# An attention and feed-forward kernel: one weight row loaded between the two loads of x, the first projection begun on half of the tiles, and the tiles of x evacuated by halves on two engines

## The chip, the cores and the metric

One core of a Trainium2 chip. The time is the device time of one execution in microseconds (us). The kernel is long tuned: about 287 us, of which the change touches the first fifteen. Medians and ranges are of all runs (one of the kernel before, 290.98 us, counts as slow). A ratio is the mean time of one kernel's fast runs over the mean of the other's fast runs of the same rounds, so it is not quite the ratio of the medians that are quoted.

## The reference

```python
# x: (1, 2048, 640) bf16; 32 heads of 20; F = 1728
qkv = x @ wqkv                                   # (640, 1920): q, k, v
pq, pk = q @ w_phi, k @ w_phi                    # by head, 20 x 20
phi = concat(softmax(p), softmax(-p))            # for q and k
kv, z = phi_k^T @ v, sum(phi_k)
a = (phi_q @ kv) / (phi_q @ z + 1e-6) @ wo
b = (gelu(x @ w_gate) * (x @ w_up)) @ w_down
g = sigmoid((x * gate_w).sum(-1))
out = g * a + (1 - g) * b
```

## The kernel before

TensorE needs x transposed (`xT`, 16 tiles of 128 tokens). The first four tiles are loaded as they are (`xtok`, two loads of two tiles) and transposed on TensorE into PSUM, from where VectorE and ScalarE copy ("evacuate") them to `xT`; the other twelve are transposed by the DMA engines. Then v is projected for these four tiles, one "v step" per tile and row block of the weights (five row blocks `w3[:, kt]`, each 160 KB, called v rows here). After that come v of tiles 4 and 5, the folding of `w_phi` into the weights of k and q, and everything else.

```python
# loads(): all on one queue (SyncE), in this order
        xload("sp", 0)                      # tiles 0 and 1, 320 KB
        xload("sp", 2)                      # tiles 2 and 3, 320 KB
        for kt in range(KD):                # v rows 0 to 4, 160 KB each
            sc.dma("sp", lambda e: e.dma_start(self.w3[:, kt, 0:D], w3[:, kt, 2 * D:3 * D]), writes=[("wv", kt)])
        xturn(4, 2)                         # DMA transposes: x tiles 4, 5
        wload(self.wkT, D, "wkT")           # k's weights
        xturn(6, 2)                         # x tiles 6, 7
        wload(self.wqT, 0, "wqT")
# x_transpose(t, ek): ten 64-row transposes, then ONE evacuation by DVE or ACT
        if ek == "a":
            sc.op("act", lambda e: e.activation(out, src, AF.Copy), reads=rd, writes=[("xT", t)])
        else:
            sc.op("dve", lambda e: e.tensor_copy(out, src), reads=rd, writes=[("xT", t)])
# attention_state(): TensorE's order
        for n in (512, 512, 512, 512, 512, 512, 128, 128, 128):
            ...                             # dummy matmuls until x lands
        xt(0, "d"); xt(1, "a")
        ...                                 # six dummy matmuls
        xt(2, "d"); xt(3, "a")
        for kt in range(4):                 # (written out in the kernel)
            for t in range(4):
                vs(t, kt)
        self.blockdiag()
        self.gate_column(6)
        for t in range(4):
            vs(t, 4)
            ...                             # evacuate v: 480 columns per tile, tails together
        ve(4, 6); ve(5, 0)                  # v of tiles 4, 5
        f(0, "k", (2, 3), "d"); f(1, "k", (4, 5), "a")   # folds of k ...
```

The softmax here doesn't subtract the row's maximum and nothing guards it: scores larger than these inputs give would overflow.

Of the kernel before, what the change touches and what calls it, by code (L numbers as in the profile page):

```python
# [3 lines left out]
P = 128  # L4
BF16 = mybir.dt.bfloat16
F32 = mybir.dt.float32
AF = mybir.ActivationFunctionType
# [100 lines left out]
class _Kernel:  # L108
    S, D, H, DH, F = 2048, 640, 32, 20, 1728
    KD = D // P  # L110
# [97 lines left out]
    def loads(self):  # L208
        sc, nc = self.sc, self.nc
        D, KD, DH, P_ = self.D, self.KD, self.DH, P  # L210
        w3 = self.wqkv.rearrange("(kt p) n -> p kt n", p=P)
# [3 lines left out]
        def xload(q, j):  # L215
            sc.dma(q, lambda e: e.dma_start(self.xtok[:, j:j + 2, :], x4[:, j:j + 2, :]),
                   writes=[("xtok", j), ("xtok", j + 1)])

        def wload(T, c0, key):
            sc.dma("sp", lambda e: e.dma_start_transpose(T[:, :, :], self.wqkv[:, c0:c0 + D]), writes=[key])  # L220

        def xturn(t, n):
# [5 lines left out]
              writes=["gtmp"])  # L228
# [2 lines left out]
                                                compare_op=ALU.not_equal, fill=1.0, base=0, channel_multiplier=1),  # L231
              writes=["ident"])
        xload("sp", 0)
        xload("sp", 2)
        for kt in range(KD):
            sc.dma("sp", lambda e: e.dma_start(self.w3[:, kt, 0:D], w3[:, kt, 2 * D:3 * D]), writes=[("wv", kt)])
        xturn(4, 2)
        wload(self.wkT, D, "wkT")
        xturn(6, 2)
        wload(self.wqT, 0, "wqT")  # L240
        xturn(8, 4)
        xturn(12, 4)
# [11 lines left out]
        for r in (0, 1):  # L254
            sc.dma("sp", lambda e: e.dma_start(self.wd_sb[64 * r:64 * r + 64, 13, :], self.wd[13 * P:self.F, :]),
                   writes=[("wd13", r)])
        sc.dma("sp", lambda e: e.dma_start(self.wo_sb[:, :, :], self.wo.rearrange("(kt p) n -> p kt n", p=P)),
               writes=["wo"])
# [3 lines left out]
        for i in range(KD):  # L262
            n = self.HHI[i] - self.HLO[i] + 1
# [11 lines left out]
            reads=[("mask", 1)], writes=["wphi"])  # L275
# [10 lines left out]
        for s in range(self.NSV):  # L286
            pool(lambda e, s=s: e.memset(self.vaug[:, s, :, DH:self.DA], 1.0), [("vone", s)])

    def x_transpose(self, t, ek):

        sc = self.sc
        b, w = (0, 4, 2, 6)[t], self.D // 2
        bks = (b, b + 1)
        pv = self.bank(b, 1024).bitcast(BF16).rearrange("p (r c) -> p r c", r=2)[:, :, 0:w]
        for c in range(self.KD):
            for r in (0, 1):
                a = 64 * r
                sc.op("pe", lambda e: e.transpose(  # L298
                    pv[:, r, c * 64:(c + 1) * 64], self.xtok[a:a + 64, t, c * P:(c + 1) * P],
                    self.ident[a:a + 64, a:a + 64]),  # L300
                    reads=[("xtok", t), "ident"], writes=[("ps", bks[r])], signal=(c == self.KD - 1))
        out = self.xT[:, :, t * P:(t + 1) * P].rearrange("p c (r t) -> p c r t", t=64)
        src = pv.rearrange("p r (c t) -> p c r t", t=64)
        rd = [("ps", b) for b in bks]
        if ek == "a":
            sc.op("act", lambda e: e.activation(out, src, AF.Copy), reads=rd, writes=[("xT", t)])
        else:
            sc.op("dve", lambda e: e.tensor_copy(out, src), reads=rd, writes=[("xT", t)])

    def blockdiag(self):  # L310
        DH = self.DH
# [56 lines left out]
                    kt == self.KD - 1, [("xT", t)] + [(k, kt) if k != "wgate" else k for k in keys])  # L368

    def v_step(self, t, kt):  # L370
        sc = self.sc
        for c0, n, bk, col in ((0, 480, t, 0), (480, 160, 4 + t // 3, 160 * (t % 3))):
            sc.op("pe", lambda e, c0=c0, n=n, bk=bk, col=col: e.matmul(  # L373
                self.bank(bk)[:, col:col + n], self.xT[:, kt, t * P:(t + 1) * P], self.w3[:, kt, c0:c0 + n],
                start=(kt == 0 and col == 0), stop=(kt == self.KD - 1), skip_group_check=True),
                reads=[("xT", t), ("wv", kt)], writes=[("ps", bk)], signal=(kt == self.KD - 1))

    def v_first_evac(self, ts, ek, tail):
        sv, nt = ts[0], len(ts)
        h0, nh = (24, 8) if tail else (0, 24)  # L380
        dst = self.vaug[:, sv:sv + nt, h0:h0 + nh, 0:self.DH]
        bk = 4 + ts[0] // 3 if tail else ts[0]
        src = self.bank(bk, nt * nh * self.DH).rearrange("p (t h d) -> p t h d", t=nt, d=self.DH)
        rd = [("ps", bk)] + [("vone", t) for t in ts]
        wr = [("vaug", t) if tail else ("vmain", t) for t in ts]
        if ek == "d":
            self.sc.op("dve", lambda e: e.tensor_copy(dst, src), reads=rd, writes=wr)
        else:
            self.sc.op("act", lambda e: e.activation(dst, src, AF.Copy), reads=rd, writes=wr)

    def k_early(self, t, b0):
        self.proj(t, 640, 384, b0, 128, ["wk2"])
# [70 lines left out]
    def gram(self, t):  # L463
        sc = self.sc
        se, sv = t % self.NSE, t % self.NSV
        va = self.vaug[:, sv, :, :].rearrange("p h c -> p (h c)")
        for g, a, b, c, lo, f0, nf in self.gram_groups():
            sc.op("pe", lambda e: e.matmul(  # L468
                self.ps[a:a + 64, b * 512 + c:b * 512 + c + 2 * nf], va[:, lo:lo + 64], self.Ek[:, se, :, f0:f0 + nf],
                start=(t == 0 and g in (0, 1, 8, 9)), stop=(t == self.NT - 1 and g in (6, 7, 9, 10)),  # L470
                skip_group_check=True),
                reads=[("Ek", se, 0), ("Ek", se, 1), ("vaug", sv), ("vmain", sv), ("vone", sv)], writes=[("ps", b)],
                signal=(g in (7, 10)))

    def kv_evac(self):
# [75 lines left out]
    def attention_state(self):  # L551
        NT = self.NT
        order = [(b, i) for b in range(self.NB) for i in range(self.KD)]
        sc = self.sc
        ones = self.nc.const_aps.tensor(1.0, [P, 512], BF16)
        for n in (512, 512, 512, 512, 512, 512, 128, 128, 128):
            sc.op("pe", lambda e: e.matmul(self.bank(0, n), ones[:, 0:P], ones[:, 0:n], start=True, stop=True),  # L557
                  writes=[("ps", 0)])
        vs, ve, xt = self.v_step, self.v_first_evac, self.x_transpose
        xt(0, "d")  # L560
        xt(1, "a")
        for i in range(3):
            for a, b in ((0, 2), (64, 3)):
                sc.op("pe", lambda e: e.matmul(self.bank(b, P), ones[a:a + 64, 0:P], ones[a:a + 64, 0:P], start=True,  # L564
                                               stop=True), writes=[("ps", b)])
        xt(2, "d")
        xt(3, "a")
        for t in range(4):
            vs(t, 0)
        for t in range(4):  # L570
            vs(t, 1)
        for t in range(4):
            vs(t, 2)
        for t in range(4):
            vs(t, 3)
        self.blockdiag()
        self.gate_column(6)
        for t in range(4):
            vs(t, 4)
            ve([t], "ad"[t % 2], False)  # L580
            if t == 2:
                ve([0, 1, 2], "a", True)
        ve([3], "d", True)
        f = self.fold
        ve, ke = self.v_early, self.k_early
        ve(4, 6)
        ve(5, 0)
        f(0, "k", (2, 3), "d")
        f(1, "k", (4, 5), "a")
        f(2, "k", (6, 7), "d")  # L590
        f(3, "k", (0, 1), "a")
        f(4, "k", (2, 3), "d")
        ve(6, 4)
        ke(0, 6)
        self.k_sums(0)
        ve(7, 0)
        ke(1, 2)
        f(0, "q", (4, 5), "d")
        f(1, "q", (6, 7), "d")
        ke(2, 0)  # L600
        f(2, "q", (4, 5), "d")
        f(3, "q", (2, 3), "d")
        self.proj(3, 640, 384, 6, 128, ["wk2"])
        f(4, "q", (4, 5), "d")
        self.proj(3, 1024, 257, 7, 0, ["wk2", "wgate"])
        self.k_evac(3, 6)
        self.k_scale(0)
        self.k_norm(1)
        self.pq(0, 1, 1, 0)
        self.pq(0, 0, 0, 1)  # L610
        self.pq(0, 3, 3, 2)
        self.columns = True
        self.gram(0)
        self.k_norm(2)
        self.pq(0, 2, 2)
        self.k_norm(3)
        n = 4
        g = 1
        for t in range(4, NT):
            if t < 8:  # L620
                self.k_early(t, 1)
            else:
                self.vk(t)
            self.k_norm(t)
            m = 2 * t - 2 if t < 8 else t + 5
            while n < m:
                if n == m - 1:
                    for g in range(g, t - 2):
                        self.gram(g)
                    g = t - 2  # L630
                self.pq(order[n][0], order[n][1], n)
                n += 1
# [83 lines left out]
    def down_pair(self, t0, banks, widths):  # L716
# [63 lines left out]

    NUMB = 2
    oldk = [("Ek", k, r) for k in range(4) for r in (0, 1)] + [(w, k) for w in ("Dk", "Rk") for k in range(4)] + [
        (w, k) for w in ("vaug", "vmain", "vone") for k in range(8)]
    oldw = [(w, k) for w in ("wv", "wk2", "wq2") for k in range(5)] + ["wgate"]

    def ffn(self):
# [88 lines left out]
```

## Time and profile before

| | |
|---|---|
| time, first three runs | 286.37, 287.10, 290.98 us |
| span of the profiled execution (286.25 us) | 285.0 us |
| TensorE busy | 281.1 us |
| first v step | 5.28 us |
| first fold of k | 13.54 us |

The page of the kernel before; the first lines are busy time with its share of the span, the last ones the chain of work that ended last, by engine and by line:

```profile
span 285.0 us, 7066 instructions
PE 281.1 (99%) x3045; PEld 186.1 (65%) x3060; DVE 174.4 (61%) x352; ACT 105.2 (37%) x200; POOL 5.3 (2%) x36
...
PE 99%; issue 0%; ACT 0%
PE ps L361 62%; PE ps L737 28%; PE ps L681 2%; PE ps L373 2%; PE ps L468 2%; PE ps L341 1%; PE ps L557 1%; PE ps L298 0%; ACT outsb L750 0%; PE ps L564 0%; PE ps L323 0%
```

TensorE (PE) is the chain.

The timeline of TensorE in the opening of the kernel before. Columns: start, duration, engine, line, operation, what it writes and reads, shapes, how many merged into the row, and in brackets the idle time before it with what ended it:

```profile
3.81 0.71 PE L298 MATMUL ps<-ident,xtok 64*128 64x64 bf16 x20
4.34 0.51 PE L564 MATMUL ps<-const-bfloat16-1.0 64*128 64x128 bf16 x6
4.70 0.53 PE L298 MATMUL ps<-ident,xtok 64*128 64x64 bf16 x20
5.28 4.56 PE L373 MATMUL ps<-w,xT 128*128 128x480 bf16 x32
```

Transposes of tiles 0 and 1 at 3.81, dummies, transposes of tiles 2 and 3 at 4.70, v from 5.28: no bracket, so no long wait. And the view of the tile `xtok`, the two loads of x and their times to landing:

```profile
L216 SPq DMA_DIRECT2D xtok<-in_A_x_dram x2: 408/410/413, 0.8 to 1.3; - x2
...
DMA to landing us min/median/max: 2.9/3.2/3.4
```

The first load is issued at 0.80 and lands at 3.72, the second is issued at 1.27 and lands at 4.66 (the landing times of single transfers are in the trace). The v rows land at 5.15, 5.75, 6.32, 6.91 and 7.39.

### The profile page before, as it was taken

To read this page: it belongs to the slowest core of one execution; us is meant where nothing else is said; L and a number is where in the kernel's file an instruction comes from. 1 tells how busy PE (TensorE), PEld (TensorE's weight loads), DVE (VectorE), ACT (ScalarE), POOL (GpSimd) and SP (SyncE) were. 2 spreads that over 40 slices of the span, in tenths; PEclk is the share of its full clock that TensorE was granted. 3 is DMA by queue.
4 is the path that set the end of the run, shared out by engine and by line. 5 is a ranking of instruction groups with operands and counts; after the bars stand their busy time and mean duration, and the time that the engine had idled before them with its cause. 6 is when DMAs were issued, how large, how long until landed. Compare 5 with 4: busy or idle time off the path is not lost.

```text
span 285.0 us, 7066 instructions
## 1 busy us (share of the span) xinstructions
PE 281.1 (99%) x3045; PEld 186.1 (65%) x3060; DVE 174.4 (61%) x352; ACT 105.2 (37%) x200; POOL 5.3 (2%) x36
## 2 busy tenths in 40 slices
PE   8999999999999999999999999999999999999996
PEld 4665799999984444444444444445777777777786
DVE  1459999999976652667242334225883883883801
ACT  4367898667754223222322223221112112112021
POOL 7000000000000000000000000000000000000000
DMA  8999993000002000011000000000233223322421
GB/s 228 225 199 313 361 349 111 2 0 2 2 0 48 0 0 2 2 23 25 0 0 0 2 0 0 0 2 0 26 82 58 50 62 59 70 52 68 71 72 48
DMA packets 36937, 18.67 MB, mean 66 GB/s; under 512 B 28970, under 2 KB 36394, under 8 KB 36906
## 3 DMA queue, kind: packets, MB, share of 16 engines
q1 hardware_dynamic: 36240, 18.19, 26.3%
q8 instruction: 24, 0.39, 0.6%
q10 hardware_dynamic: 666, 0.03, 0.2%
q14 instruction: 7, 0.06, 0.1%
HBM read 9.04 MB, written 2.62 MB: 41 GB/s over the span
## 4 chain that ended last, share of the span: by engine, by line
PE 99%; issue 0%; ACT 0%
PE ps L361 62%; PE ps L737 28%; PE ps L681 2%; PE ps L373 2%; PE ps L468 2%; PE ps L341 1%; PE ps L557 1%; PE ps L298 0%; ACT outsb L750 0%; PE ps L564 0%; PE ps L323 0%
## 5 line engine op out<-in xcount | busy, mean ns | idle before, releaser
L361 PE MATMUL ps<-xT,wg_sb 128*128 128x512 bf16 (+1 forms) x265 | 63.8, 379 | 0.4 <-issue 0.2
L361 PE MATMUL ps<-xT,wu_sb 128*128 128x512 bf16 (+1 forms) x263 | 63.3, 379 | 0.4
L653 ACT ACTIVATE gl<-ps 128x512 bf16<-128x512 f32 x52 | 30.9, 596 | 72.9 <-PE ps L361 70.7
L655 DVE TENSOR_TENSOR hT<-ps,gl 128x512 bf16<-128x512 f32 x39 | 26.6, 689 | 38.8 <-PE ps L361 38.7
L737 PE MATMUL ps<-wd_sb,hT 64*128 64x320 bf16 x648 | 48.5, 296 | 0.0
L361 PEld LDWEIGHTS ps<-xT,wu_sb 128*128 128x128 bf16 (+1 forms) x270 | 26.6, 99 | 29.5
L361 PEld LDWEIGHTS ps<-xT,wg_sb 128*128 128x128 bf16 (+1 forms) x270 | 26.2, 99 | 29.0 <-ACT gl L653 0.2
L361 PE MATMUL ps<-w,xT 128*64 128x512 bf16 (+6 forms) x398 | 41.5, 325 | 0.1
L750 ACT ACTIVATE outsb<-ps,Gm 128x320 bf16<-128x320 f32 (+2 forms) x31 | 14.5, 515 | 72.4 <-PE ps L737 72.4
L737 PEld LDWEIGHTS ps<-wd_sb,hT 64*128 64x128 bf16 x648 | 31.1, 94 | 12.2 <-issue 0.4
L361 PEld LDWEIGHTS ps<-w,xT 128*64 128x64 bf16 (+1 forms) x400 | 35.9, 107 | 4.5
L737 PE MATMUL ps<-wo_sb,goT 64*128 64x320 bf16 (+2 forms) x340 | 26.5, 288 | 0.0
L361 PE MATMUL ps<-xT,wq 128*64 128x512 bf16 (+1 forms) x184 | 26.0, 380 | 0.1
L438 DVE TENSOR_REDUCE Dk<-Ek 128x64 f32<-128x1280 bf16 x16 | 23.7, 1478 | 3.7 <-ACT gcol L426 3.7
L452 DVE TENSOR_TENSOR Ek<-Ek,Dk 128x640 bf16<-128x640 bf16 x32 | 25.0, 821 | 0.6
L708 DVE TENSOR_TENSOR O<-ps,RH 128x640 bf16<-128x640 f32 x32 | 24.7, 815 | 0.0
L423 ACT ACTIVATE Ek<-ps 128x640 bf16<-128x640 f32 x32 | 20.7, 703 | 4.2 <-PE ps L361 4.2
L537 ACT ACTIVATE Eq<-ps 128x512 bf16<-128x512 f32 x40 | 21.6, 607 | 0.6 <-PE ps L361 0.4
L655 DVE TENSOR_TENSOR xT<-ps,gl 128x512 bf16<-128x512 f32 x13 | 9.0, 690 | 18.2 <-PE ps L361 18.2
L737 PEld LDWEIGHTS ps<-wo_sb,goT 64*128 64x128 bf16 x340 | 16.0, 94 | 5.3
L361 PEld LDWEIGHTS ps<-xT,wq 128*64 128x64 bf16 (+1 forms) x185 | 15.4, 108 | 2.9
L737 PE MATMUL ps<-wd_sb,xT 64*128 64x320 bf16 (+2 forms) x270 | 16.0, 269 | 0.0
(71 smaller groups left out, 173.8 us busy)
## 6 DMA issues: line engine op xcount, KB each, us to landing
out_dram<-outsb SPq DMA_DIRECT2D x7, 320.0 KB, 2.3
wd_sb<-in_B_w_down_dram SPq DMA_DIRECT2D x1, 2080.0 KB, 12.9
wg_sb<-in_B_w_gate_dram SPq DMA_DIRECT2D x1, 1120.0 KB, 7.4
wu_sb<-in_B_w_up_dram SPq DMA_DIRECT2D x1, 1120.0 KB, 9.8
wg_sb<-in_B_w_gate_dram SPq DMA_DIRECT2D x1, 960.0 KB, 9.1
wu_sb<-in_B_w_up_dram SPq DMA_DIRECT2D x1, 960.0 KB, 9.3
w<-in_A_wqkv_dram SPq DMA_DIRECT2D x5, 160.0 KB, 3.6
wo_sb<-in_A_wo_dram SPq DMA_DIRECT2D x1, 800.0 KB, 8.5
```

The lines of the kernel that those rows point to most:

```text
L361: self.sc.op("pe", lambda e: e.matmul(self.ps[a:z, bank * 512 + c0:bank * 512 + c0 + n], lhs[:, a:z], rhs, start=first, stop=fin), reads=r ...
L373: sc.op("pe", lambda e, c0=c0, n=n, bk=bk, col=col: e.matmul(self.bank(bk)[:, col:col + n], self.xT[:, kt, t * P:(t + 1) * P], self.w3[:, ...
L423: self.sc.op("act", lambda e, s=s, scale=scale: e.activation(self.Ek[:, se, s, :], self.ps[:, o:o + self.D], AF.Exp, scale=scale), reads=[ ...
L438: sc.op("dve", lambda e: e.tensor_reduce(self.Dk[:, se, 0, :].rearrange("p (s h) -> p s h", h=H), self.Ek[:, se, :, :].rearrange("p s (h d ...
L452: sc.op("dve", lambda e, v=v, r=r: e.tensor_tensor(v, v, r, ALU.mult), reads=[("Rk", se)], writes=[("Ek", se, s)])
L468: sc.op("pe", lambda e: e.matmul(self.ps[a:a + 64, b * 512 + c:b * 512 + c + 2 * nf], va[:, lo:lo + 64], self.Ek[:, se, :, f0:f0 + nf], st ...
L537: sc.op("act", lambda e, s=s, scale=scale: e.activation(self.Eq[:, s, i, b * self.BT:(b + 1) * self.BT], self.bank(bank), AF.Exp, scale=sc ...
L653: sc.op("act", lambda e: e.activation(self.gl[:, slot, :], self.bank(banks[0]), AF.Gelu_apprx_tanh), reads=[("ps", banks[0])], writes=[("g ...
L655: sc.op("dve", lambda e: e.tensor_tensor(hT, self.bank(banks[1]), self.gl[:, slot, :], ALU.mult), reads=[("ps", banks[1]), ("gl", slot)], ...
L708: dve(lambda e, o=o, f=f, s=s: e.tensor_tensor(o, V[s][:, :, :, 0:DH], f, ALU.mult), rb + [key(6 + s)], [("O", s, sl)], guard=old)
L737: sc.op("pe", lambda e: e.matmul(self.bank(bk, w), lhs, rhs, start=opens and x == 0, stop=end and not opens, skip_group_check=True), reads ...
L750: sc.op("act", lambda e: e.activation(dst, self.bank(bk, w), AF.Copy, scale=g), reads=rd, writes=wr)
```

## The change

The intent: do not wait for tiles 2 and 3. v row 0 is loaded between the two loads of x, so that the first v steps of tiles 0 and 1 run while tiles 2 and 3 arrive. Each tile is evacuated in two halves, left on VectorE and right on ScalarE, so that it is ready sooner. Each tile now has its own pair of PSUM banks for v and one evacuation, and the gate column (the weights of the gate `g`, transposed on TensorE and copied into the weights by VectorE) moves behind tile 5, when a bank is free.

```diff
         xload("sp", 0)
+        vload(0)
         xload("sp", 2)
-        for kt in range(KD):
-            sc.dma("sp", ...v row kt...)
+        for kt in range(1, KD):
+            vload(kt)
...
-        if ek == "a":
-            sc.op("act", ...whole tile...)
-        else:
-            sc.op("dve", ...whole tile...)
+        for r in (0, 1):
+            if r:
+                sc.op("act", ...half r..., reads=[("ps", 2 * t + r)], writes=[("xTh", t, r)])
+            else:
+                sc.op("dve", ...half r..., reads=[("ps", 2 * t + r)], writes=[("xTh", t, r)])
...
-        xt(2, "d")
-        xt(3, "a")
-        (v rows 0 to 3, each over tiles 0 to 3)
-        self.blockdiag()
-        self.gate_column(6)
-        (v row 4 with v_first_evac)
+        vs(0, 0)
+        vs(1, 0)
+        xt(2)
+        xt(3)
+        for ts, k in (((0, 1), 1), ((2, 3), 0), ((2, 3), 1), (range(4), 2)):
+            for t in ts:
+                vs(t, k)
+        self.blockdiag()
+        for t in range(4):
+            vs(t, 3)
+            vs(t, 4)
+            self.v_evac(t, 2 * t, "ad"[t % 2])
-        ve(4, 6)
-        ve(5, 0)
+        ve(4, 0)
+        ve(5, 2)
+        self.gate_column(4)
 (the folds and later steps: other bank numbers, same order)
```

## The prediction

> What bounds the kernel now. The chain of waits is 99% TensorE, and the page shows TensorE busy 281.1 of 285.0 us. Any gain must make TensorE start useful work earlier or wait less; what the opening gains or loses should pass to the end. VectorE is about 98% busy from 25 to 77 us (busy time by stretch), but it starts from TensorE's output and shifts with it. The change touches about 3.8 to 15 us.
>
> The opening before (timeline, single instructions, landing times of the DMA issues):
> - x of tiles 0 and 1 lands at 3.72, of tiles 2 and 3 at 4.66; v rows at 5.15, 5.75, 6.32, 6.91, 7.39; the transposed wk at 12.84 and it is first used at 13.49.
> - Transposes of tiles 0, 1: 3.81 to 4.34 (issue). Dummy matmuls to 4.70. Transposes of tiles 2, 3: 4.70 to 5.07 (issue); their spacing falls from 53 to 29 ns at about 4.87, where the fast clock comes on.
> - v starts at 5.28 and its 20 tile-steps (about 0.27 us each, 5.44 in all) end at 10.99, with the gate column's transpose inside. TensorE idles only 0.2 to 0.3 us between 4.70 and 11: no long wait for the change to fill.
>
> What the change does, with durations from the trace:
> - DMA: v row 0 lands at about 4.2 to 4.3, x of tiles 2 and 3 at 5.15, the rest unchanged.
> - Evacuation by halves: VectorE took 0.49 us and ScalarE 0.70 for 640 elements. From other lengths in the trace (ScalarE 0.57 for 480, 0.18 for 1; VectorE 0.18 for 5) a half is an estimated 0.34 on VectorE, 0.44 on ScalarE. ScalarE must do all four right halves. Tile 0 is ready at about 4.85, tile 1 at 5.3 (before: 4.89, 5.36).
> - TensorE: dummies to 4.70; wait 0.2; v(0,0); wait 0.1; v(1,0) to about 5.6; transposes of tiles 2, 3 now all at the fast clock, 0.29 instead of 0.37 to 0.5; row 1 for tiles 0, 1 to 6.45; then tiles 2 and 3 wait for ScalarE's halves, an estimated 0.1 to 0.2 each; end of v about 11.0 to 11.1, against 10.99.
> - So 0.54 us of v moves ahead, but almost all of it is returned as short waits for ScalarE.
> - The gate column's transpose moves behind tile 5 and its VectorE copy (0.18, about 0.5 with the semaphores) now holds bank 4, which fold 1 of k needs some 0.4 us later: an estimated wait of 0.1 to 0.2.
>
> Sum: between 0.3 us earlier and 0.5 later, centre 0.1 to 0.2 later. That is inside the spread of the three runs (286.4, 287.1, and 290.98, likely slow).
>
> Predicted 287.1 us, 80% range 286.2 to 288.1. Faster by over 2%: 1%; within 2%: 98%; slower by over 2%: 1%.
>
> What would show the steps right: v's first matmul at 4.8 to 5.0; new TensorE waits on xT (ScalarE) at the first uses of tiles 1, 2, 3; tile 4's v starting within 0.3 us of 11.0; a short wait of fold 1 for the gate copy; the rest of the trace the same, shifted.
>
> What would make it wrong: the new gaps could keep the clock slow longer. The Trainium skill, "TensorE: Matmul & The Clock Gate", Part 1, says the full clock needs one busy window of about 3.4 us; the trace agrees roughly (matmuls from 0.84, fast at 4.87). [...]

## The result, and the profile after

Median 287.55 us (287.28 to 287.73, six runs) against 286.82 us (286.37 to 290.98, six runs); ratio 1.0028, with a 95% interval of 1.0014 to 1.0041. It is slower beyond the noise, by about 0.8 us between the means of the fast runs. (The medians differ by 0.7 us, the figure used below; that of the kernel before includes its slow run.)

The page of the changed kernel:

```profile
span 286.1 us, 7067 instructions
PE 281.3 (98%) x3044; PEld 185.7 (65%) x3060; DVE 174.8 (61%) x353; ACT 105.2 (37%) x201; POOL 5.3 (2%) x36
...
PE 97%; DMA 2%; issue 1%; SPq 0%; ACT 0%
PE ps L362 63%; PE ps L716 28%; PE ps L660 2%; PE ps L453 2%; DMA xtok<-in_A_x_dram 2%; PE ps L342 1%; PE ps L299 0%; SPq L216 0%; SPq L220 0%; ACT outsb L729 0%; PE ps L324 0%
```

TensorE's busy time is the same. A new name stands in the chain: the load of `xtok` (x of tiles 0 to 3). The chain again, in order of time, up to 12 us (start, duration, what):

```profile
1.73 4.49 DMA xtok<-in_A_x_dram
6.22 0.05 issue
6.27 0.47 PE ps L299 x20
6.73 0.21 issue
6.94 5.09 PE ps L362 x36
```

The second load of x is issued at 1.73 and lands at 6.22. The chain runs through it: everything from 6.27 on waited for it. The timeline of TensorE in the changed kernel:

```profile
3.83 0.72 PE L299 MATMUL ps<-ident,xtok 64*128 64x64 bf16 x20
4.36 0.51 PE L549 MATMUL ps<-const-bfloat16-1.0 64*128 64x128 bf16 x6
4.88 0.81 PE L362 MATMUL ps<-w,xT 128*128 128x512 bf16 x4
6.27 0.47 PE L299 MATMUL ps<-ident,xtok 64*128 64x64 bf16 x20 [0.57 <-DMA xtok<-in_A_x_dram]
6.94 0.44 PE L362 MATMUL ps<-w,xT 128*128 128x128 bf16 x2 [0.21 <-issue]
```

The intent is met: two v steps (four matmuls) run from 4.88, 0.40 us earlier than before. Then the wait of 0.57 us, marked with its cause. (0.57 is counted from the modelled end of the last matmul; from the moment at which a further matmul could have started, 5.53, it is 0.74.) The row at 6.94 seems to wait for "issue"; in truth the record of the 512-column matmul ahead of it is missing, which must have started at about 6.73, just after v row 1 had landed (6.67).

The view of the tile `xtok` in the changed kernel; the maximum is the second load, 1.1 us more than before:

```profile
L216 SPq DMA_DIRECT2D xtok<-in_A_x_dram x2: 412/423/434, 0.8 to 1.7; - x2
...
DMA to landing us min/median/max: 3.0/3.7/4.5
```

| landing, us | before | changed |
|---|---|---|
| x, tiles 0 and 1 | 3.72 | 3.79 |
| v row 0 | 5.15 | 4.15 |
| x, tiles 2 and 3 | 4.66 | 6.22 |
| v rows 1 to 4 | 5.75 to 7.39 | 6.67 to 8.24 |

The account, from single instructions of the two traces: v starts 0.40 us earlier; its first step runs partly at half clock (+0.10); the wait for x of tiles 2 and 3 (+0.74); their transposes now lie within v (+0.27); the wait for v row 1 (+0.15). That is +0.86 us, and the first fold of k starts at 14.43 instead of 13.54 (+0.89). From there the two traces run nearly in parallel (the products `phi_k^T @ v` start at 29.41 and 28.44). In this account the two waits for DMA, 0.89 us together, are the whole loss: without them an estimated 0.03 us would have been gained. So the change had little to win here even with perfect landings, since the transposes that it moves into v take back 0.27 of the 0.40 us. The spans differ by 1.1 us; the last 0.2 us are gathered in two later places that were not traced to a cause. The timed medians differ by 0.7 us rather than 1.1, because the profiled execution of the kernel before (286.25 us) was one of its fastest.

### The profile page after: what moved, and what is told of

It is laid out like the page before. It is cut to its first block, busy times and chain, and to the rows that moved or that the text cites. A ratio compares the mean times of both kernels' runs of the same rounds, so it can differ in the third digit from the quotient of the medians.

```text
span 286.1 us, 7067 instructions
## 1 busy us (share of the span) xinstructions
PE 281.3 (98%) x3044; PEld 185.7 (65%) x3060; DVE 174.8 (61%) x353; ACT 105.2 (37%) x201; POOL 5.3 (2%) x36
## 4 chain that ended last, share of the span: by engine, by line
PE 97%; DMA 2%; issue 1%; SPq 0%; ACT 0%
PE ps L362 63%; PE ps L716 28%; PE ps L660 2%; PE ps L453 2%; DMA xtok<-in_A_x_dram 2%; PE ps L342 1%; PE ps L299 0%; SPq L216 0%; SPq L220 0%; ACT outsb L729 0%; PE ps L324 0%
## 5 line engine op out<-in xcount | busy, mean ns | idle before, releaser
L362 PE MATMUL ps<-w,xT 128*64 128x512 bf16 (+6 forms) x437 | 47.3, 323 | 0.3 <-issue 0.2
L362 PEld LDWEIGHTS ps<-w,xT 128*64 128x64 bf16 (+1 forms) x440 | 38.8, 106 | 7.3 <-issue 0.4
```

The source lines that it names most:

```text
L362: self.sc.op("pe", lambda e: e.matmul(self.ps[a:z, bank * 512 + c0:bank * 512 + c0 + n], lhs[:, a:z], rhs, start=first, stop=fin), reads=r ...
```

## The experiments

Theory A: the loss is the late landing of x of tiles 2 and 3, brought about by the order of the loads. Theory B: it is the halves on ScalarE, the moved gate column and the other parts that touch TensorE's order. Later theories: TensorE's clock (it starts at half speed and turns full at a moment that differs between executions), and the landing of the transposed weights of k. (In the expectations "tile 4 at 11.87 and about 11.0" were misread: tile 4's v starts at 11.65 in the changed kernel and at 10.82, inferred across a lost record, in the kernel before. The comparisons below use the first fold instead.)

### 1. The changed kernel, loads put back (run twice)

```diff
         xload("sp", 0)
-        vload(0)
         xload("sp", 2)
-        for kt in range(1, KD):
+        for kt in range(KD):
             vload(kt)
```

> The changed kernel with one part undone: both x loads first, then the five v rows, as in the kernel before. Theory A (the changed kernel loses because x of tiles 2 and 3 lands late, at 6.22 us instead of 4.66): x of tiles 2, 3 lands at 4.6 to 4.8, v row 0 at about 5.15, TensorE's wait of about 0.7 us before the transposes of tiles 2, 3 goes, v of tile 4 starts at 11.0 to 11.3 us (11.87 in the changed kernel, about 11.0 in the kernel before), and the ratio to the kernel before falls from 1.0028 to 0.999 to 1.001. Theory B (the loss is the waits for ScalarE's halves and the moved gate column, whatever the loads do): tile 4 still starts at 11.6 or later and the ratio stays at 1.002 to 1.003.

Measured: 287.55 us (287.29 to 289.12), ratio 1.003 (1.001 to 1.0051). x of tiles 2 and 3 landed at 4.55, as theory A has it, but the time did not come back (first fold at 14.50). The timeline of TensorE of this run shows why:

```profile
5.18 1.23 PE L361 MATMUL ps<-w,xT 128*128 128x512 bf16 x4 [0.33 <-ACT xT L306]
6.34 0.47 PE L298 MATMUL ps<-ident,xtok 64*128 64x64 bf16 x20
```

x is there, but in this order TensorE stands at v(0), which needs v row 0 (landed at 5.04), and idles 0.33 us. (The bracket names ScalarE, but what had just ended there, at 5.09, is the half of tile 1; that of tile 0, which v(0) needs, had ended at 4.76.) Then the four matmuls of v(0) and v(1) take 1.23 us instead of 0.81: they run at half clock (a 512-column matmul every 0.43 us with its 128-column partner 0.11, against 0.215 and 0.055), and the trace's clock record starts with the full clock only at 6.36 us. So undoing one part leaves a kernel with a wait of its own. The Trainium skill, "TensorE: Matmul & The Clock Gate", Part 1, says that the clock is decided by a window of 3413 ns that runs freely, so that the moment of full clock differs from run to run; the traces here agree: 3.84 to 6.36 us where a record exists. That the wait brought the late clock about is not shown: the stretch of 3.41 us before 6.36 holds the wait of 0.33 us, and the clock rose at its end all the same.

The second trace of the same kernel, on another chip:

> The same kernel as the first run with the loads put back, for a second trace, because its ratio of 1.003 was not what theory A expected and the late-start pair left it open. Clock theory: the gap of 0.3 us in which TensorE waits for v row 0 falls into the window that decides on the clock; this trace again shows v(0), v(1) at half clock or the clock turning full after 5.2 us. Landing theory: the clock is full at 5.2 us and the first fold waits for wk, landing at 14.0 us or later. If neither shows and the first fold stands at 13.9 to 14.1 us, the first trace was an unlucky one and times of 286.7 to 287.0 us turn up.

Measured: 287.37 us (286.92 to 289.12), ratio 1.003 (1.0003 to 1.0057).

```profile
5.35 1.02 PE L361 MATMUL ps<-w,xT 128*128 128x512 bf16 x4 [0.50 <-DMA w<-in_A_wqkv_dram]
6.30 0.47 PE L298 MATMUL ps<-ident,xtok 64*128 64x64 bf16 x20
```

Again a wait for v row 0 (landed at 5.21), here 0.50 us, and again v(0) and v(1) at half clock almost to their end. wk landed at 12.87, long before the first fold at 14.46, so the landing theory is out for this trace. The half clock is what the clock theory expected, but it may again be the moment of that execution. Some of its times (286.92, 287.02) were lower than any of the changed kernel.

### 2. The kernel before, with the new order of loads alone

The same three lines of loads as in the change, nothing else.

> The kernel before with only the order of loads changed: v row 0 between the two x loads; the order of TensorE's work is untouched, so v begins only after all four tiles are transposed. Theory A: x of tiles 2, 3 lands at about 6.2 us, transposes of tiles 2, 3 wait 1.5 us, v starts near 6.8 instead of 5.28, the ratio is 1.004 to 1.006. Bytes alone (an estimate from the landings in the trace of before: the same bytes had landed at 5.15): x lands at 5.1 to 5.3, the ratio is 1.001 to 1.002. Theory B: ratio within 0.001 of 1.

Measured: 288.32 us, ratio 1.005 (1.0027 to 1.0073). The six times form two groups: 287.44, 287.54, 287.62 and 289.02, 289.05, 289.12. The chain of this run up to 12 us:

```profile
1.73 4.28 DMA xtok<-in_A_x_dram
6.01 0.05 issue
6.06 0.47 PE ps L302 x20
```

The order of the loads alone makes x of tiles 2 and 3 land at 6.01, and the chain runs through it. Theory B is out as the whole story. The upper group, 1.5 us higher, has no trace. TensorE idles here from 4.53 to 6.06; an execution in which the clock falls back after that gap would run one stretch of 3.41 us at half clock, which costs an estimated half of it at most. The trace of this run stood near that edge: its stretch from 4.03 to 7.44 was idle for 1.53 us and the clock stayed full, while in experiment 9 a stretch that was idle for 1.54 us was followed by half clock. That fits, and is argued, not shown.

### 3. The kernel before, with the evacuation by halves alone

```diff
-        if ek == "a":  (whole tile on ACT)
-        else:          (whole tile on DVE)
+        for r in (0, 1):
+            if r:  (right half on ACT)
+            else:  (left half on DVE)
```

> The kernel before with only the evacuation of x changed: each tile in two halves, left on VectorE, right on ScalarE. Theory A: the halves are no cost: tile 1 is ready at about 5.1 instead of 5.36, the wait of 0.19 us before tile 1's first v step goes; v of tile 4 starts 0 to 0.2 us earlier; ratio 0.999 to 1.000. Theory B: ScalarE must do four halves, tiles 1 and 3 come later, v of tile 4 starts 0.2 to 0.4 us later, ratio 1.001 to 1.002.

Measured: 286.58 us (286.40 to 288.71) against 286.89; ratio 1.0007 (0.9982 to 1.0033), which one run of 288.71 pulls up. The only wait on `xT` in the kernel before, 0.19 us for ScalarE's evacuation of tile 3 at 6.12 (the expectation put it at tile 1), is gone from the list of waits. In this trace the halves make no wait, but v of tile 4 did not start earlier either (10.86 against 10.82). From the times, neither a small gain nor a loss of up to 0.9 us (the end of the interval) can be excluded.

### 4. The changed kernel again

> The changed kernel once more, unedited, for a second trace. If the late landing belongs to the order of the loads, x of tiles 2, 3 lands again at 5.9 to 6.5 us and TensorE waits 0.4 to 1.0 us for it. If it was chance (a few slow DMA packets of 0.5 to 1.0 us in one execution), it lands at 5.1 to 5.4 here and the loss must come from elsewhere. Ratio again 1.0014 to 1.0041.

Measured: 287.37 us (287.28 to 287.75), ratio 1.002 (1.0007 to 1.0032). x of tiles 2 and 3 landed at 5.92, v row 1 at 6.55; the first fold started at 14.29. TensorE waited for both again:

```profile
5.96 0.47 PE L299 MATMUL ps<-ident,xtok 64*128 64x64 bf16 x20 [0.24 <-DMA xtok<-in_A_x_dram]
6.59 7.80 PE L362 MATMUL ps<-w,xT 128*128 128x512 bf16 x56 [0.17 <-DMA w<-in_A_wqkv_dram]
```

(Counted from the moment at which a further matmul could have started, the first wait is 0.40 us, the low end of what was expected.) The late landing is not chance: 6.22, 6.01 and 5.92 in three traces with this order, 4.52 to 4.66 in six with the old order and the usual start. Nor did the order only exchange two landings: the last v row, with the same bytes moved, landed at 8.01 to 8.24 in these three and at 7.39 to 7.88 in those six.

### 5. Late start: an attempt to take the clock out

```diff
+        sc.op("dve", memset scr); 12 x sc.op("dve", reciprocal scr -> scr)
         xload("sp", 0)    # reads=["go"]: waits for the eighth
         (load of w_phi)   # reads=["go2"]: waits for the twelfth
-        for n in (512, 512, 512, 512, 512, 512, 128, 128, 128):
+        for n in (512,) * 18 + (128,) * 3:
```

> The kernel before, with all loads held back about 4.3 us (twelve tiny VectorE operations on a scratch tile; the first x load waits for the eighth, the load of w_phi for the twelfth) and dummy matmuls filling the time, so that TensorE's clock is at full speed before x arrives, in every execution. Only the late-start kernels are compared with each other. Clock theory (the spread of 286.1 to 287.3 us of the kernel before is the moment at which the clock turns full, seen at 4.0 to 6.4 us in the traces so far): the six times lie within 0.4 us. Landing theory (the spread comes from when the transposed wk lands, 12.8 to 14.3 us in the traces so far, with its first use at 13.5): they spread by 0.8 us or more as before.

> The changed kernel with the same late start. If the loss is the late x of tiles 2, 3, it is there at full clock as well, and larger than the 0.7 us measured, because the kernel before has no half-clock v steps to make up: 0.9 to 1.3 us slower than the late-start kernel before, with 0.5 to 1.0 us of TensorE idle ahead of the transposes of tiles 2, 3. If the loss is an interplay with the clock, the difference falls to under 0.4 us.

> The changed kernel with both x loads first again, late start. The trace of the same edit without late start showed the first two v steps at half clock (0.53 us lost) because TensorE idles 0.33 us for v row 0 and because the clock came at 6.36 us. Clock theory: with the clock out of the way it lies 0.2 to 0.5 us above the late-start kernel before and 0.6 us or more below the late-start changed kernel. If it equals the late-start changed kernel again, the order of the loads is not what costs.

Measured: kernel before 291.67 to 292.92 (four runs), changed kernel 292.00 to 295.25 (six), changed kernel with old loads 292.85 to 293.79 (four). The control failed: the dummies ran out before x landed (1.2 to 2.2 us of idle), and the clock fell back in two of the three. Busy time of TensorE by stretch in the late-start changed kernel; columns: stretch, its length, TensorE busy and instructions, granted clock, DMA share, GB/s:

```profile
6.26:9.67 3.41, 2.11 (x35) 1.00 0.81 228
9.67:13.08 3.41, 1.34 (x25) 1.00 1.38 241
13.08:16.49 3.41, 3.41 (x13) 0.50 0.89 181
16.50:19.90 3.40, 3.40 (x26) 1.00 1.05 177
```

In the stretch from 9.67 TensorE is busy for 1.34 of 3.41 us; in the next one it is fully busy, but at clock 0.50; then the clock is full again. The steps of the clock are 3.413 us apart. The run with old loads shows the same (busy 0.84 of 3.40, then clock 0.50). As a comparison of the change the three runs are inconclusive: their spreads overlap, and the clock that they were to remove is in them. That the kernel before spread by 1.25 us, where the clock theory expected 0.4, decides nothing for the same reason. That x of tiles 2 and 3 lands late shows in the second of them too (11.28 against 9.55), with 0.64 us of idle before their transposes and a median 0.7 us above the first.

### 6. The kernel before, with the load of wk in two parts

```diff
-        wload(self.wkT, D, "wkT")
+        wload(self.wkT, D, "wkT", 0, 2)
+        wload(self.wkT, D, "wkT", 2, KD)
```

> The kernel before (usual start) with the transposing load of wk in two parts, rows 0 to 255 and 256 to 639, so that the first folds need only the first part. Landing theory: the executions in which wk lands after 13.5 us gain up to 0.7 us: the median falls by 0.2 to 0.5 us, the times lie within 0.5 us. Clock theory: median within 0.15 us of before, spread unchanged at about 1 us.

Measured: 287.42 us (286.88 to 287.73), ratio 1.0025 (1.0011 to 1.004): slower. The first part landed at 12.09, but the fold started at 13.64 as before, because v ends there. What was lost is in the list of TensorE's waits from 13 to 20 us (who waited for what: total, times, longest):

```profile
PE ps L363 <- DMA xT<-in_A_x_dram: 0.8, 1, 0.8
```

The transposing load of x tiles 6 and 7, next in the queue, landed at 16.39 instead of 13.99 and held up v of tile 6. Neither theory expected that. There is some slack: in the trace of experiment 3 this load landed at 15.42 and held nothing up, since v of tile 6 starts at 15.47 there. The spread of the kernel before stays unexplained in part.

### 7. The changed kernel, loads and order of TensorE put back

```diff
         (loads as in experiment 1)
-        vs(0, 0); vs(1, 0); xt(2); xt(3)
-        for ts, k in (((0, 1), 1), ((2, 3), 0), ((2, 3), 1), (range(4), 2)): ...
+        xt(2); xt(3)
+        for k in (0, 1, 2):
+            for t in range(4):
+                vs(t, k)
```

> The changed kernel with both the loads and the order on TensorE put back: transposes of tiles 2 and 3 ahead of the first v step, v rows 0 to 2 over all four tiles; what stays of the change is the evacuation of x by halves, v's banks and whole-tile evacuation, and the gate column behind tile 5. If the loss is loads plus order, nothing is left: v starts at 5.2 to 5.4 us, the first fold at 13.5 to 13.8, median within 0.25 us of before, ratio 0.999 to 1.001. If the banks, whole-tile evacuations or the gate column cost, the ratio is 1.0015 or more and the first fold at 14.0 or later with v starting at 5.3.

Measured: 287.16 us (286.68 to 287.62) against 286.78; ratio 1.0015 (0.9998 to 1.0031): in between. (One of the eleven runs of the kernel before took 1700 us; it counts as slow and is not in the ratio.) In its trace v row 0 landed late, at 5.51, and v started at about 5.65; the first fold came at 13.88. From first v step to first fold it is 8.23 us, against 8.26 in the kernel before. So in this one trace banks, whole-tile evacuations and gate column cost nothing once v runs; whether they add something small in the timed runs, the interval leaves open.

### 8. The changed kernel, second x load cut by tile

```diff
-        xload("sp", 2)
+        xload("sp", 2, 1)
+        xload("sp", 3, 1)
```

> The changed kernel with the second x load cut into one load for tile 2 and one for tile 3 (1280-byte rows instead of 2560). If the late landing comes from a few slow packets that hold one queue of 2560-byte packets up, tile 2 lands at 5.2 to 5.6 us and its transposes follow the first two v steps without a long wait; the median falls 0.3 to 0.6 us below the changed kernel. If the switch of loads as such costs about 1 us, tile 3 lands at 6.0 or later and the ratio stays at 1.002 to 1.003.

Measured: 287.44 us (286.83 to 289.38), ratio 1.0033 (1.0007 to 1.0059). Tile 2 landed at 5.25, as the first reading has it, but tile 3 at 6.00, and the ratio stayed, as the second has it. The first transposes started at 5.73, but v row 1 landed at 6.59, and TensorE waited for that instead. Lateness moved from one load to the next; no gain shows. Tile 3 has the bytes ahead of it that the uncut load had, now in packets of 1280 bytes like those of the v rows, and it was late: the size of the packets is not what makes it late here.

### 9. The changed kernel, later loads held back

```diff
         def vload(kt):
-            sc.dma("sp", ..., writes=[("wv", kt)])
+            sc.dma("sp", ..., reads=[("xtok", 2)] if kt == 1 else [], writes=[("wv", kt)])
```

> The changed kernel with the later loads held back: the queue issues v row 1 and all that follows only when x of tiles 2 and 3 has landed. A look at one landing time, not a candidate (everything later comes about 2 us late). If x is late because the rows behind it overtake it on faster queues and compete with it, it lands here at 4.9 to 5.3 us, as bytes alone would have it. If it is late because of the load of v row 0 ahead of it, whatever follows, it lands at 5.8 to 6.3 us again.

The chain of this run, up to 12 us, and then the timeline of TensorE:

```profile
1.73 3.55 DMA xtok<-in_A_x_dram
5.28 0.02 issue
5.30 0.33 SPq L220
```

```profile
4.79 0.81 PE L363 MATMUL ps<-w,xT 128*128 128x512 bf16 x4 [0.29 <-DVE xT L310]
5.53 0.47 PE L300 MATMUL ps<-ident,xtok 64*128 64x64 bf16 x20
```

With v row 0 still in front, but no row behind it, x of tiles 2 and 3 lands at 5.28, as bytes alone would have it, and its transposes follow the two v steps without a wait: what the change was meant to look like. So in this trace v row 0 in front costs about 0.6 us, which is what its bytes take, and the loads queued behind cost 0.6 to 0.9 us more in the others. (This is a single look, its state unknown. The run as a whole took 290.51 us: v row 1 now lands at 7.46, TensorE waits 1.91 us for it, and the clock is at half from 7.25 to 10.66.) The packets in the trace show what overtook it: when the last packet of x of tiles 2 and 3 was in, 362 of the 640 packets of the v rows had been moved in the changed kernel, though only the 128 of row 0 were ahead of it in the queue; in the kernel before it were 91, all of them behind it. The Trainium skill, "DMA: Bandwidth & Descriptors", Queues, rings and completion order, says that one load is split over up to 16 DMA engines, each consuming its own ring in order, so that completion is not first in, first out. The trace agrees as far as it goes: 234 packets of later rows, nearly two rows of 128, were in before the last packet of x (it does not tell which engine moved a packet). In the changed kernel four packets of this load took over 0.4 us, in experiment 9 two, in the kernel before none; why packets stall more in this order, no run shows. Nor does a run show why rows behind the third load hurt here and not before: in the old order v row 0 was the third load, with four rows behind it, and landed at 4.93 to 5.51 in six traces. The small load of `w_phi` on ScalarE's queue is no explanation: of its 640 packets 328 were in before the last of x in the changed kernel, but 504 in experiment 9.

## Why the prediction was right or wrong

The time, the range and the direction were right (predicted 287.1 us within 286.2 to 288.1, measured 287.55), the sum was too small (centre 0.1 to 0.2 us later, measured 0.7), and the waits named in it were not the ones that came. That the time still fell inside the range is luck in part: the range was 1.9 us wide, for a forecast change of 0.1 to 0.2 us, and the waits for DMA that made the loss were not in the sum.

- "what bounds the kernel": right. TensorE's busy time did not change (281.1 and 281.3 us), and the delay of the opening reached the end.
- "x of tiles 2 and 3 at 5.15, the rest unchanged": wrong, and the mis-sized term. It landed at 6.22 (5.92 in the second trace), and v rows 1 to 4 came 0.8 to 0.9 us later than before. The step that failed was to count bytes ahead in the queue. In experiment 9, with the rows behind held back, the count holds (5.28); with them it does not.
- "v row 0 lands at about 4.2 to 4.3" and "v's first matmul at 4.8 to 5.0": right, 4.15 and 4.88.
- "a half is an estimated 0.34 on VectorE, 0.44 on ScalarE": right, 0.32 and 0.44. But "tile 1 at 5.3" was wrong: it was ready at 5.11, since the second half starts 0.33 us after the first on ScalarE and overlaps it. The prediction had added durations.
- "almost all of it is returned as short waits for ScalarE": wrong. The only wait on an evacuation is the one of about 0.25 us ahead of the first v step, which the prediction had as 0.2; none follows for tiles 1, 2 and 3. The same amount and more was returned as waits for DMA, 0.74 us for x and 0.15 us for v row 1.
- "an estimated wait of 0.1 to 0.2" of fold 1 for the gate copy: not found. The folds take 1.73 us from first to last in both traces.
- "end of v about 11.0 to 11.1": wrong, 11.65 (10.82 before), and therefore tile 4 not within 0.3 us.
- The clock as a risk: real, but not the main loss here (0.10 us in this trace). It shows more in the experiments with gaps than in the change.

What is settled: the order of loads alone makes x late (experiment 2) and needs the loads queued behind to do so (experiment 9, one trace); the halves make no wait (trace of experiment 3). What is not: how much of the 0.7 us would come back with a perfect landing, because every kernel that was run to show it (experiments 1, 7, 8) had a loss of its own from the clock or from another load. So that the late x costs the 0.7 us is read from the chain and the account of one trace, and from experiment 2, but not shown by winning it back. No kernel was found that is surely faster than the kernel before.

## What to carry to other kernels

Here a load moved ahead of another delayed the other by its bytes (0.6 us) and by what was queued behind (0.6 to 0.9 us more). Where an opening depends on loads, read landing times per load, before and after, and plan with slack. Undoing one part of such a change can create a new wait instead of recovering the old time, so look at the trace of the undone kernel before judging by its time. A gap on TensorE in the first microseconds can cost twice: the gap, and half clock for the 3.41 us after it (experiments 5 and 9).

## What the Trainium skill lacked or had wrong

- "TensorE: Matmul & The Clock Gate", Why this matters for your kernels: it asks for no gaps over about 3 us and speaks of one idle window. Here a window needs not be idle: with TensorE idle in 2.07 of 3.41 us (busy 1.34) and in 2.56 of 3.41 us, the clock fell to 0.50 for the next 3.413 us (experiment 5), and so it did after a window with 1.54 us idle in experiment 9; no gap in these windows was longer than 2.23 us. With 1.53 of 3.41 us idle in one window (experiment 2) it stayed full. Idle time is counted from modelled ends, so the edge is known only roughly.
- The same page, Part 1: the window of 3413 ns and its free phase agree with the runs (half-clock stretch of 3.413 us; full clock first at 3.84 to 6.36 us in the traces with a record). What it lacks is how busy a window must be to raise the clock: the window of 3.41 us that ended at 10.66 in experiment 9 with 0.66 us idle did, the one in experiment 1 that ended at 2.95 with 1.30 us idle did not.
- The same page, Part 4, says that transposes on TensorE don't engage the full clock. Transposes alone were not tried; but transposes did run at full speed here once the clock was full (a pair every 29 ns instead of 53).
- "DMA: Bandwidth & Descriptors", Queues, rings and completion order: that completion isn't first in, first out, agrees. It gives no size for it: 234 packets of later loads were in before the last packet of x, and the landing moved from 5.28 to 5.9 to 6.2 us.
